# Causal attention feeding a mixture of experts: earlier closed pages, a copy moved to ScalarE, later row places, and dummy matmuls

## The chip, the cores and the metric

The kernel runs on one core of a Trainium2 chip. The metric is the device time in microseconds (us) of one execution. The engines are TensorE (PE; its weight loads are PEld), VectorE (DVE), ScalarE (ACT), GpSimd (POOL) and SyncE (SP, which here issues transfers).

## What is computed

Blockwise causal attention, whose output goes through a mixture of experts with one expert for each token:

```python
B, H, S, D = 8, 8, 576, 64
scores = q @ k.transpose(0, 1, 3, 2) / sqrt(D)
mask = pos[:, None] // 64 >= pos[None, :] // 64       # causal by blocks of 64
attn = softmax(where(mask, scores, -1e9))
x = (attn @ v).transpose(0, 2, 1, 3).reshape(B * S, H * D)   # 4608 tokens x 512
logits = x @ w_gate                                   # 8 experts
e = argmax(logits, axis=1); gate = softmax(logits)[e]
# tokens sorted by expert; for each expert: y = relu(x @ w1[e]) @ w2[e]
out = gate * y                                        # in the tokens' order
```

Inputs and output are float32.

## The kernel before

Attention works on pairs of heads: 4 pairs in a batch, 32 pairs in all, numbered p. Keys, queries and probabilities are turned on TensorE with fp16 operands. When a batch is done, its tokens are routed: VectorE chooses each token's expert (choose), TensorE ranks the tokens of each expert by matmuls with triangular ones, VectorE works out the row of each token (route), and GpSimd scatters the rows to a buffer in device memory, `xsorted`, that is divided into pages of 128 rows with one expert each. A page is closed when it is full. Afterwards 36 to 43 pages are fetched one by one, each multiplied by its expert's two matrices, and its rows are scattered to the output. The first 10 pages to be worked on (`FIRST`) are closed pages, so that they may start before the last batches have been scattered. TensorE's, ScalarE's and, in attention, GpSimd's orders are those of the program; VectorE's and SyncE's are set by a scheduler.

The turning of k (n = 1) and q (n = 0), with who copies them out of PSUM:

```python
def trans(p, n):
    ps = o_ps.tile([128, 640], F16, name=("o1", "o0")[n])
    for c in range(5):
        nc.tensor.transpose(ps[:, c * 128:c * 128 + 128], ...)      # L208
    copy = nc.scalar.copy if n else nc.vector.tensor_copy
    copy(qkT[:, n, 0:512]..., ps[:, 0:512]...)                      # L211
    copy(qkT[:, n, 512:576], ps[:, 512:576])                        # L213
```

`scores` (L231, L238) makes the scores of the next pair, and ScalarE their exponentials (L241, L233); `sums` adds the probabilities over keys on VectorE (L247, L253, L255); `attend` multiplies them by v (L272); `denominators` reads the sums on TensorE (L285) and copies the result (dl, L301); `finish` turns the pair's output (L315, L318) and divides it (L320 to L331). The PSUM pool `t_ps`, from which the tiles named tp of route, denominators and finish come, has two buffers.

```python
def route(b):
    nc.scalar.activation(ex, d, AF.Exp)
    rk_ps = psum_small()[:, 0:6 * E]
    nc.tensor.matmul(out=rk_ps..., lhsT=before16, rhs=oh...)        # L377
    ...                                                             # five more, L381
    nc.vector.reduce_sum(out=sm, in_=ex, axis=AX.X)
    nc.vector.reciprocal(x16.bitcast(F32)[:, :, 256], sm)
    nc.vector.tensor_copy(rk..., rk_ps)                             # L388
    # some 20 operations on 128x8 and 128x40 on VectorE, L392 to L429:
    # counts, pages, rows (slot), the last open pages (lastA), pages used

def scatter(b, j):                      # 128 rows of 1032 bytes
    if b == B - 2:
        nc.gpsimd.memset(spare, 0.0)
    ins = nc.gpsimd.indirect_dma_start(out=xsorted[:, :], ...)      # L442
    (early if b < B - 1 else late).append(ins.ins.name)
    ...
```

The loop over the pairs (cut), and what follows it:

```python
load(0), load(1), load_v(0), gate_weights()
for n in range(8):
    nc.tensor.matmul(out=idle[:, 0, 0:128], lhsT=ident32, rhs=ident32, ...)   # L566
cast(0); trans(0, 0); trans(0, 1); cast(1)
for t in range(4): scores(0, t)
for n in range(2): trans(1, n)
...
for p in range(PAIRS):
    load_v(p + 2); load(p + 3); cast(p + 2)
    if p == 1: route_constants()
    sums(p)
    scores(p + 1, 0); scores(p + 1, 1)
    ...                                           # scatters of the last batch
    attend(p, (0, 1), 0); attend(p, (0, 1), 1); attend(p, (2, 3, 4), 1)
    scores(p + 1, 2); scores(p + 1, 3)
    trans(p + 2, 1); trans(p + 2, 0)
    if p > HP and p % HP == 1: route(p // HP - 1)
    if p == PAIRS - 2: first_places()
    if p == PAIRS - 1: orders()                   # order1, L535
    denominators(p)
    ...                                           # scatters, load_weights
    if p: finish(p - 1)
    if p >= HP and p % HP == 0: choose(p // HP - 1)
    if p == PAIRS - 3: closed()
    if p == PAIRS - 2: free_rows()
load_weights(4 * E - 2); load_weights(4 * E - 1)  # 512 KB each, L124
for e in range(E): fill_rows(e)                   # L477
...
for T in range(5): mload(T)                       # fetch page T, L666
mtx(0)                                            # turn page 0, L676, L680
for T in range(ends[0] - 1): step(T, ends[0])

def mload(T):
    xs = xsp.tile([128, ROW], I32, name="xs")     # in the memory of the probabilities
    page = number(T, 0, ET.SP, NP - 1)            # from order1 for T < FIRST
    ins = nc.sync.dma_start(out=xs, in_=xs_pages[:, ds(page, 1), :]...)
    wait_for(ins, early if T < FIRST else early + fills + late)

def step(T, n):                                   # cut
    m1(T)                                         # first matrix, L692, relu L697
    if T == 0: finish(PAIRS - 1, yps); choose(B - 1)
    if T == 1: route(B - 1); scatters of batch 7; last_experts()
    if T == 3: last_order()
    mtx(T + 1); mth(T - 1); m2(T - 2)             # L704, L714; scale L717, scatter L718
```

Of the kernel before, what the change touches and what calls it, by code (L numbers as in the profile page):

```python
# [22 lines left out]
def kernel(  # L23
# [10 lines left out]
    nc = tc.nc  # L34
# [29 lines left out]

    FIRST = 10
# [7 lines left out]
    cnt, pages, lastA, used = (consts.tile([128, w], F32, name=n) for n, w in (  # L73
        ("cnt", E), ("pages", E), ("lastA", E), ("used", 1)))
# [14 lines left out]
    def constants():  # L89
        nc.gpsimd.memset(fill, 0)  # L90
        nc.gpsimd.iota(fill[:, 257:258], pattern=[[0, 1]], base=NO_TOKEN,
                       channel_multiplier=0)
    def route_constants():
        make_upper_triangular(nc, before16, 1.0, diag=False)
        nc.gpsimd.memset(ones16, 1.0)
        nc.gpsimd.memset(ione, 1.0)
        place_i = place.bitcast(I32)
        pref_i = pref.bitcast(I32)
        nc.gpsimd.iota(pref_i, pattern=[[0, 5], [-1, E]], base=E, channel_multiplier=0)
        nc.gpsimd.tensor_copy(pref, pref_i)  # L100
        nc.gpsimd.iota(page_i, pattern=[[0, 1]], base=0, channel_multiplier=1)
        nc.gpsimd.tensor_copy(page_f, page_i)
        nc.gpsimd.iota(place_i, pattern=[[1, NP]], base=0, channel_multiplier=0)
        nc.gpsimd.tensor_copy(place, place_i)
        nc.gpsimd.tensor_copy(page_h, page_f)
        nc.gpsimd.tensor_scalar(row_m, page_f, -128.0, None, op0=ALU.add)
        nc.gpsimd.tensor_scalar(row_n, page_f, -float(NO_TOKEN), None, op0=ALU.add)
        nc.gpsimd.memset(em_all, 0.0)
        for t in (cnt, pages, lastA, used):
            nc.gpsimd.memset(t, 0.0)  # L110
# [17 lines left out]
    with tc.tile_pool(name="ld", bufs=2) as ld, \  # L128
# [73 lines left out]
        def trans(p, n):  # L202
            if ("qkT", p) not in st:
                st["qkT", p] = c16.tile([128, 2, 576], F16, name="qkT")
            qkT = st["qkT", p]
            ps = o_ps.tile([128, 640], F16, name=("o1", "o0")[n])
            for c in range(5):
                nc.tensor.transpose(ps[:, c * 128:c * 128 + 128],  # L208
                                    h16[:, n, c].rearrange("p h d -> p (h d)"), ident16)
            copy = nc.scalar.copy if n else nc.vector.tensor_copy  # L210
            copy(qkT[:, n, 0:512].rearrange("d (p c) -> d p c", c=4),  # L211
                 ps[:, 0:512].rearrange("d (c p) -> d p c", c=4))
            copy(qkT[:, n, 512:576], ps[:, 512:576])  # L213
# [158 lines left out]
        def route(b):  # L372
            d, x16, oh = st.pop(("d", b)), st.pop(("x16", b)), ohs[b % 2]
# [6 lines left out]
            for s in range(1, 6):  # L380
# [3 lines left out]
            sm = small("sm", 5)  # L384
            nc.vector.reduce_sum(out=sm, in_=ex, axis=AX.X)
            nc.vector.reciprocal(x16.bitcast(F32)[:, :, 256], sm)
            rk = rp.tile([128, 6, E], F32, name="rk")
            nc.vector.tensor_copy(rk.rearrange("p j e -> p (j e)"), rk_ps)  # L388

            cnt2, pages2, new, inc, base, pb, tmp = (  # L390
                small(n) for n in ("cnt2", "pages2", "new", "inc", "base", "pb", "tmp"))
# [27 lines left out]
            nc.vector.tensor_copy(slot, sl)  # L419
            st["slot", b], st["x16", b] = slot, x16  # L420
# [7 lines left out]
            nc.vector.tensor_copy(cnt, cnt2)  # L428
            nc.vector.tensor_copy(pages, pages2)  # L429
# [6 lines left out]
        def scatter(b, j):  # L436

            slot, x16 = st["slot", b], st["x16", b]
            m = 128 if j < 4 else 64
            if b == B - 2:  # L440
                nc.gpsimd.memset(spare, 0.0)
            ins = nc.gpsimd.indirect_dma_start(  # L442
                out=xsorted[:, :],
                out_offset=bass.IndirectOffsetOnAxis(ap=slot[0:m, j:j + 1], axis=0),
                in_=x16[0:m, j, :], in_offset=None)
            (early if b < B - 1 else late).append(ins.ins.name)
            if b < B - 1:
                apart("rows", ins)
            else:

                wait_for(ins, fills)
                apart("end rows", ins)
                tc.add_to_no_dep_group("last rows", ins.ins)

        def free_rows():

            got, w = small("got"), small("frw")
            nc.vector.scalar_tensor_tensor(out=got, in0=pages, scalar=-128.0, in1=cnt,
# [26 lines left out]
        def closed():  # L485

            cur, hit = small("cur"), small("hit")
            opn, cl = small("opn", 1), small("cl", 1)
# [69 lines left out]
        with tc.manual_schedule(engines={ET.PE, ET.Activation, ET.Pool}):  # L558
# [5 lines left out]
            idle = s_ps.tile([128, 2, 512], F32, name="s")  # L564
            for n in range(8):
                nc.tensor.matmul(out=idle[:, 0, 0:128], lhsT=ident32, rhs=ident32, start=True,  # L566
                                 stop=True)
            cast(0)
            for n in range(2):
                trans(0, n)  # L570
            cast(1)
            for t in range(4):
                scores(0, t)
            for n in range(2):
                trans(1, n)
            load(2)
# [3 lines left out]
            for p in range(PAIRS):  # L580
# [11 lines left out]
                sums(p)  # L592
                if nxt:
                    scores(p + 1, 0)
                    scores(p + 1, 1)
                if p == PAIRS - 2:
                    scatter(B - 2, 0)
                    scatter(B - 2, 1)
                elif p == PAIRS - 1:
                    scatter(B - 2, 4)  # L600
                elif p > HP and p % HP in (2, 3):
                    scatter(p // HP - 1, 2 * (p % HP - 2))
                if p > HP + 1 and p % HP == 0:
                    scatter(p // HP - 2, 4)
# [11 lines left out]
                if p == PAIRS - 2:  # L616
                    first_places()
                if p == PAIRS - 1:
                    orders()
                denominators(p)  # L620
                if p == PAIRS - 2:
                    scatter(B - 2, 2)
                    scatter(B - 2, 3)
                elif p > HP and p % HP in (2, 3) and p < PAIRS - 2:
                    scatter(p // HP - 1, 2 * (p % HP - 2) + 1)
                if 2 < p < PAIRS - 2:
                    for n in range(((p - 3) * 30 + 26) // 27, ((p - 2) * 30 + 26) // 27):
                        load_weights(n)
                if p:
# [4 lines left out]
                if p == PAIRS - 3:  # L634
                    with tc.high_priority():
                        closed()
# [3 lines left out]
            load_weights(4 * E - 2)  # L640
            load_weights(4 * E - 1)
# [7 lines left out]
        yps.extend(t_ps.tile([128, Dm], F32, name="tp") for _ in range(2))  # L649
# [13 lines left out]
        def mload(T):  # L663
# [4 lines left out]
            if T < FIRST:  # L668
                tc.declare_no_dep(ins.ins, group="last rows", reason="pages closed before")
# [56 lines left out]
        def step(T, n):  # L726
# [5 lines left out]
            if T == 1:  # L732
                route(B - 1)
                for j in range(5):
# [33 lines left out]
        with tc.manual_schedule(engines={ET.PE, ET.Activation}):  # L768
            for T in range(5):
                mload(T)  # L770
            mtx(0)
            for T in range(ends[0] - 1):
# [35 lines left out]
```

## Time and profile before

| | before |
|---|---|
| median of 3 runs | 418.81 us (418.07 to 419.86) |
| span of the profile | 418.9 us |
| PE busy | 385.4 us (92%) |
| PEld busy | 241.8 us (58%) |
| DVE busy | 237.1 us (57%) |
| ACT busy | 212.4 us (51%) |
| POOL busy | 198.7 us (47%) |
| mean granted TensorE clock | 0.976 |

In the lines of the profile, L272 is line 272 of the kernel. A line of the timeline has the start in us, the time in us from the first to the last of the merged instructions, engine, line, operation, out<-in, how many, and in brackets how long the engine was idle before and what ended that wait. SPq is the queue of SyncE, which issues transfers. A slice of the page is a fortieth of the span; its digit is the busy share in tenths. Attention takes the span from its start to about 237 us, the experts the rest.

### The profile page before, as it was taken

What the parts mean: (1) busy time and instruction counts of PE and PEld (TensorE: products, weight loads), DVE (VectorE), ACT (ScalarE), POOL (GpSimd) and SP (SyncE); (2) the same over time, 40 slices, a digit from 0 to 9 for tenths busy, and PEclk for the clock granted to TensorE, in tenths of its full rate; (3) what the DMA queues carried; (4) which work ended last, traced back from release to release, by engine and by line L of the source; (5) the groups of instructions that cost most, each with busy time, mean ns of one, the idle gap of its engine ahead of it and who ended that gap; (6) DMA issues with size and microseconds to landing.
All of it is one profiled execution on the core that took longest, in us unless ns stands there. A gap on an engine that the chain in (4) does not pass through costs nothing.

```text
span 418.9 us, 11629 instructions
## 1 busy us (share of the span) xinstructions
PE 385.4 (92%) x4110; PEld 241.8 (58%) x4110; DVE 237.1 (57%) x767; ACT 212.4 (51%) x341; POOL 198.7 (47%) x400
## 2 busy tenths in 40 slices
PE   5999989999999899999998648999999999999993
PEld 4557656667666566576665424555555555555551
DVE  1466898897988888969889607232323232222220
ACT  4666756666667566575666002344444434343441
POOL 3565467657476676765773840612121212121212
PEclk9699999999999999999999959999999999999998
DMA  6786999989989899999894570332223222322222
GB/s 165 230 228 174 224 245 198 240 192 239 236 198 271 210 231 256 254 210 255 186 220 87 103 201 0 121 115 89 102 77 101 78 102 80 112 89 89 81 90 76
DMA packets 83067, 67.58 MB, mean 161 GB/s; under 512 B 52079, under 2 KB 75375, under 8 KB 83008
## 3 DMA queue, kind: packets, MB, share of 16 engines
q0 software_dynamic: 9824, 31.31, 32.6%
q1 hardware_dynamic: 72352, 34.89, 31.0%
q8 instruction: 37, 0.61, 0.6%
q10 hardware_dynamic: 832, 0.59, 0.5%
q14 instruction: 22, 0.18, 0.2%
HBM read 67.56 MB, written 17.23 MB: 202 GB/s over the span
## 4 chain that ended last, share of the span: by engine, by line
PE 30%; issue 28%; DVE 14%; DMA 12%; POOL 11%; ACT 2%; SPq 1%; POOLq 1%; ACTq 0%
PE o L272 14%; POOL out_dram L718 8%; PE tp L285 6%; DMA out_dram<-y,xs 4%; PE s L238 4%; DMA wall<-in_moe_w_dram 4%; PE o L208 2%; PE tp L318 2%; PE tp L315 2%; DVE acc L247 2%; DVE x L326 2%; DVE acc L253 2%; POOL xsorted L477 2%; DVE acc L255 1%; DMA qk<-in_k_dram 1%
## 5 line engine op out<-in xcount | busy, mean ns | idle before, releaser
L241 ACT ACTIVATE pt<-s 128x1024 f32<-128x1024 f32 x96 | 94.9, 1025 | 48.2 <-issue 26.9
L272 PE MATMUL o<-pt,v 128*64 128x320 f32 (+3 forms) x768 | 91.7, 389 | 0.0
L718 POOL DMA_INDIRECT out_dram<-y,xs x38 | 37.4, 983 | 111.0 <-ACT y L717 108.1
L680 DVE COPY xsT<-o 128x512 f16<-128x512 f16 x38 | 16.1, 423 | 105.9 <-PE o L676 105.8
L692 PE MATMUL s<-wall,xsT 128*128 x304 | 73.5, 386 | 2.6 <-DMA xsorted<-fill,frows 1.2
L272 PEld LDWEIGHTS o<-pt,v 128*64 128x64 f32 x768 | 50.9, 139 | 36.6 <-issue 7.3
L714 PE MATMUL tp<-wall,hT 128*128 x304 | 71.7, 379 | 0.0
L697 ACT ACTIVATE h<-s 128x1024 f16<-128x1024 f32 x38 | 38.9, 1023 | 58.5 <-PE s L692 58.5
L442 POOL DMA_INDIRECT xsorted<-x,slot x40 | 44.9, 1122 | 30.1 <-DVE em_i L504 14.1
L717 ACT ACTIVATE y<-tp,xs 128x512 f32<-128x512 f32 x38 | 26.1, 687 | 53.4 <-PE tp L714 53.4
L243 POOL MEMSET pt<- 64x128 f32 x128 | 23.8, 202 | 61.7 <-ACT pt L241 49.0
L692 PEld LDWEIGHTS <-xsT 128*128 128x128 f16 x304 | 30.1, 99 | 39.1 <-issue 2.6
L198 POOL CAST qk<-qk 128x512 f16<-128x512 f32 x62 | 44.9, 745 | 8.9 <-DMA qk<-in_q_dram 5.3
L714 PEld LDWEIGHTS <-hT 128*128 128x128 f16 x304 | 28.4, 99 | 27.1
L276 ACT COPY oT<-o 128x256 f32<-128x256 f32 x64 | 25.7, 402 | 32.6 <-PE o L272 32.6
L247 DVE TENSOR_TENSOR acc<-pt 128x896 f32<-128x896 f32 x32 | 38.2, 1195 | 2.4 <-POOL pt L243 2.4
L211 DVE COPY qkT<-o 128x512 f16<-128x512 f16 x32 | 21.9, 686 | 25.4 <-PE o L208 25.4
L238 PE MATMUL s<-qkT 64*128 64x512 f16 (+4 forms) x320 | 32.5, 298 | 2.6 <-ACT qkT L211 1.7
L285 PE MATMUL tp<-acc,picks 128*32 128x128 f32 (+1 forms) x512 | 28.3, 265 | 3.7 <-DVE acc L255 1.7
L326 DVE TENSOR_TENSOR x<-tp,rec 128x512 f16<-128x512 f32 x64 | 31.1, 485 | 0.0
L707 DVE COPY hT<-o 128x1024 f16<-128x1024 f16 x38 | 26.2, 690 | 7.3 <-PE o L704 4.8
L253 DVE TENSOR_TENSOR acc<-acc,pt 128x640 f32<-128x640 f32 x32 | 28.2, 882 | 0.0
(155 smaller groups left out, 545.8 us busy)
## 6 DMA issues: line engine op xcount, KB each, us to landing
wall<-in_moe_w_dram POOLq DMA_DIRECT2D x32, 512.0 KB, 7.4
qk<-in_q_dram SPq DMA_DIRECT2D x32, 256.0 KB, 4.5
v<-in_v_dram SPq DMA_DIRECT2D x64, 128.0 KB, 5.9
qk<-in_k_dram SPq DMA_DIRECT2D x30, 256.0 KB, 5.0
xs<-xsorted SPq DMA_DIRECT2D x43, 129.0 KB, 2.0
xsorted<-fill SPq DMA_DIRECT2D x1, 1419.0 KB
tl<-in_q_dram SPq DMA_DIRECT2D x32, 32.0 KB, 6.3
v<-in_v_dram SPq DMA_DIRECT2D x32, 32.0 KB, 5.9
```

What stands on the lines that cost most here:

```text
L198: eng.tensor_copy(h16[:, n, 0:4].rearrange("p c h d -> p h c d"), qk[:, n].rearrange("p h (c d) -> p h c d", c=4))
L238: nc.tensor.matmul(out=sp[:, h, o:o + w], lhsT=qkT[r, 1, c * 128:c * 128 + 128], rhs=qkT[r, 0, q0:q0 + w], start=True, stop=True)
L241: nc.scalar.activation(pt[:, :, t * 512:t * 512 + 512], sp, AF.Exp, scale=scale)
L247: ins = nc.vector.tensor_tensor(out=acc[:, :, 0:448], in0=pt[:, :, 128:576], in1=pt[:, :, 576:1024], op=ALU.add)
L272: nc.tensor.matmul(out=o[h * 64:h * 64 + 64, q0 - lo:hi - lo], lhsT=vt[:, c, h, :], rhs=src, start=(c == 0), stop=(c == last), skip_group_ ...
L285: nc.tensor.matmul(out=ps[32 * t:32 * t + 32, cols], lhsT=lhsT, rhs=src, start=start, stop=True, skip_group_check=True)
L326: nc.vector.tensor_tensor(out=x16[:, j:j + n, hp * 128:hp * 128 + 128].rearrange("p i (h d) -> p i h d", h=2), in0=rows.rearrange("p (i h ...
L442: ins = nc.gpsimd.indirect_dma_start(out=xsorted[:, :], out_offset=bass.IndirectOffsetOnAxis(ap=slot[0:m, j:j + 1], axis=0), in_=x16[0:m, ...
L692: nc.tensor.matmul(out=hp[:, half * 512:half * 512 + 512], lhsT=xT[:, c * 128:c * 128 + 128], rhs=weight(T, 2 * c + half), start=(c == 0), ...
L697: nc.scalar.activation(h, hp, AF.Relu)
L714: nc.tensor.matmul(out=yp, lhsT=hT[:, f * 128:f * 128 + 128], rhs=weight(T, 8 + f), start=(f == 0), stop=(f == 7))
L718: ins = nc.gpsimd.indirect_dma_start(out=out[:, :], out_offset=bass.IndirectOffsetOnAxis(ap=xs[:, 257:258], axis=0), in_=y, in_offset=None ...
```

## The change

It does five things. The first ten pages are those closed when batch 5 (of 0 to 7) has its places, not batch 6: `closed`, `first_places` and `orders` move three to four pairs forward, and batch 6's scatters are no longer waited for by the first ten fetches. ScalarE, not VectorE, copies the turned q from pair 2 on, and also the ranks. The row places become a function of their own, `places`, a pair behind the ranks, with counts and pages in two buffers in turn so that two copies fall away. A batch's five scatters go three in one pair and two in the next, where they were two, two and one; the weights are issued ahead of the attention of a pair, two in each of the last three pairs, where the last two came behind the loop. And single dummy matmuls are put between the first transposes and scores, into a tile of `t_ps`. The finish of pair 30 moves behind the turning of the first page. It is meant to take waits away where attention gives way to the experts, to take work from VectorE where it is fullest, and to keep TensorE's clock up at the start.

The diff, cut:

```diff
+    cnts, pagess = ([consts.tile([128, E], F32, name=f"{n}{i}") for i in range(2)]
+                    for n in ("cnt", "pages"))
@@ constants(), ahead of the loop; was in route_constants(), in pair 1
+        for t in (cnts[0], pagess[0], lastA, used):
+            nc.gpsimd.memset(t, 0.0)
@@ trans
-            copy = nc.scalar.copy if n else nc.vector.tensor_copy
+            copy = nc.scalar.copy if p > 1 or n else nc.vector.tensor_copy
@@ route
-            sm = small("sm", 5)
-            nc.vector.reduce_sum(out=sm, in_=ex, axis=AX.X)
-            nc.vector.reciprocal(x16.bitcast(F32)[:, :, 256], sm)
             rk = rp.tile([128, 6, E], F32, name="rk")
-            nc.vector.tensor_copy(rk.rearrange("p j e -> p (j e)"), rk_ps)
+            nc.scalar.copy(rk.rearrange("p j e -> p (j e)"), rk_ps)
+            st["rk", b] = rk, ex
+
+        def places(b):
 ... the operations on places, with sm and its reciprocal behind slot
-            nc.vector.tensor_copy(cnt, cnt2)
-            nc.vector.tensor_copy(pages, pages2)
@@ scatter
-            if b == B - 2:
+            if b < B - 1:
                 nc.gpsimd.memset(spare, 0.0)
-            (early if b < B - 1 else late).append(ins.ins.name)
+            (early if b < B - 2 else late).append(ins.ins.name)
             if b < B - 1:
                 apart("rows", ins)
+                if b == B - 2:
+                    tc.add_to_no_dep_group("last rows", ins.ins)
@@ start
-            idle = s_ps.tile([128, 2, 512], F32, name="s")
-            ... 8 dummy matmuls
+            idle = t_ps.tile([128, 512], F32, name="tp")
+            warm(8)
             cast(0)
             for n in range(2):
                 trans(0, n)
+                warm(1)
             cast(1)
             for t in range(4):
                 scores(0, t)
+                warm((0, 2, 1, 0)[t])
             for n in range(2):
                 trans(1, n)
+            warm(1)
@@ loop, after sums(p)
+                if p > HP and p % HP == 2:
+                    places(p // HP - 1)
@@ loop, after scores(p + 1, 1)
-                ... two scatters at p % HP == 2 and 3, one at 0, here and after denominators
+                if p > HP and p % HP == 3:
+                    scatter(p // HP - 1, 0)
+                    scatter(p // HP - 1, 1)
                 if p > HP + 1 and p % HP == 0:
-                    scatter(p // HP - 2, 4)
+                    scatter(p // HP - 2, 3)
+                if p > 2:
+                    first = p - 3 + max(0, p - PAIRS + 3)
+                    for n in range(first, first + 1 + (p >= PAIRS - 3)):
+                        load_weights(n)
@@ loop, around denominators(p)
-                if p == PAIRS - 2:
+                if p == PAIRS - 5:
                     first_places()
-                if p == PAIRS - 1:
+                if p == PAIRS - 4:
                     orders()
                 denominators(p)
+                if p > HP and p % HP == 3:
+                    scatter(p // HP - 1, 2)
+                if p > HP + 1 and p % HP == 0:
+                    scatter(p // HP - 2, 4)
-                if p:
+                if 0 < p < PAIRS - 1:
                     finish(p - 1)
-                if p == PAIRS - 3:
-                    with tc.high_priority():
-                        closed()
+                if p == PAIRS - 6:
+                    closed()
@@ behind the loop
-            load_weights(4 * E - 2)
-            load_weights(4 * E - 1)
+            for j in (3, 4):
+                scatter(B - 2, j)
             for e in range(E):
                 fill_rows(e)
@@ experts
             if T == 1:
                 route(B - 1)
+                places(B - 1)
@@
             mtx(0)
+            finish(PAIRS - 2)
+            yps.extend(t_ps.tile([128, Dm], F32, name="tp") for _ in range(2))
```

## The prediction

> **What bounds the kernel now.** I read the page's 40 slices first, then the busy time by stretch, then the timeline of the stretches where TensorE is not busy. The page gives TensorE 92% of the span, so only stretches in which it idles or runs at a lower granted clock, and pairs longer than its own work, can yield time.
>
> ```profile
> PE   5999989999999899999998648999999999999993
> PEclk9699999999999999999999959999999999999998
> ```
>
> There are two places with both faults: slices 1 and 2, and slices 23 to 25. By stretch (us, then busy us and count of PE, PEld, DVE, ACT, POOL, then clock, DMA share, GB/s):
>
> ```profile
> 10.00:16.80 6.80, 6.04 (x36) 3.45 (x37) 3.08 (x5) 4.20 (x8) 4.09 (x21) 0.50 0.68 175
> 238.70:242.10 3.40, 0.00 (x0) 0.00 (x0) 0.02 (x1) 0.00 (x0) 2.85 (x6) 1.00 1.06 212
> 242.10:252.30 10.20, 5.95 (x23) 3.50 (x23) 0.74 (x4) 1.02 (x1) 4.14 (x7) 0.50 0.60 180
> 98.26:104.75 6.49, 6.49 (x96) 4.51 (x94) 5.00 (x14) 4.53 (x9) 4.89 (x11) 1.00 1.06 228
> 104.75:112.07 7.32, 6.88 (x102) 4.77 (x100) 6.83 (x27) 4.63 (x10) 4.15 (x12) 1.00 1.09 233
> 112.07:119.40 7.33, 7.07 (x95) 4.63 (x93) 6.93 (x34) 4.55 (x9) 3.86 (x8) 1.00 0.91 228
> ```
>
> The reader is to see: half clock for 6.8 us at the start; 3.4 us with TensorE wholly idle between attention and experts and then 10.2 us at half clock; and three neighbouring pairs of heads, a plain one of 6.49 us, all TensorE, and two of 7.3 us in which VectorE is at 93 to 95%. The plain pair is the floor; the two long ones carry choose and route. The timeline of the change from attention to experts says why TensorE stops:
>
> ```profile
> 235.39 0.17 DVE L535 CAST order<-tp 1x20 int32<-1x20 f32 x1
> 235.50 1.18 POOL L124 DMA_DIRECT2D wall<-in_moe_w_dram  x2
> 237.28 9.22 SPq L666 DMA_DIRECT2D xs<-xsorted  x10
> 245.15 0.61 PE L676 MATMUL o<-ident,xs 128*128 128x128 f16 x4 [7.72 <-DMA xs<-xsorted]
> 246.96 3.57 PE L692 MATMUL s<-wall,xsT 128*128 x8 [1.20 <-DMA xsorted<-fill,frows]
> ```
>
> The first page is fetched only after the order of pages is known (L535) and batch 6's rows have been scattered; the fetch goes out at 237.28, behind 1 MB of weights issued at 235.5, and TensorE waits until 245.15. At the start, one more wait, and one pair's ScalarE against TensorE for later:
>
> ```profile
> 24.88 0.17 DVE L405 SCALAR_TENSOR_TENSOR room<-pages,cnt 128x8 f32<-128x8 f32 x1 [3.53 <-POOL pages L110]
> 25.84 0.41 PE L285 MATMUL tp<-acc,picks 128*32 128x128 f32 x2 [0.79 <-DVE acc L253]
> 102.61 0.27 ACT L233 ACTIVATE pf<-s 64x128 f32<-64x128 f32 x1
> 102.91 0.58 ACT L211 COPY qkT<-o 128x512 f16<-128x512 f16 x1
> 103.39 0.22 ACT L213 COPY qkT<-o 128x64 f16<-128x64 f16 x1
> 104.69 1.94 ACT L241 ACTIVATE pt<-s 128x1024 f32<-128x1024 f32 x2 [1.09 <-issue]
> 104.21 0.61 PE L238 MATMUL s<-qkT 64*128 64x512 f16 x6
> ```
>
> **What the Trainium skill says.** "TensorE: Matmul & The Clock Gate", Part 1, has the array's clock halved after an idle window of about 3.4 us and restored after a busy one, in free-running windows. The trace agrees: half clock comes in stretches of 6.8 and 10.2 us, two and three such windows. It shows more: the window of 6.6 to 10.0 us, which ended in the first half clock, had TensorE busy about 1.4 us (0.4 before 7.0, 0.61 at 7.67, 0.40 at 9.17), so some 42% was not enough. "DMA: Bandwidth & Descriptors", section "Issuing engines are not separate DMA queues", says that all transfers share the same 16 engines: the trace has the page fetches (129 KB) landing in 2.0 us at the median of the whole run, but in 6.0 us here beside the weights, with the DMA share at 1.06.
>
> **The change part by part.**
>
> *Start.* Six dummy matmuls go into the first gaps. The first eight took 3.79 us, 0.47 each, and six of 0.47 lie in gaps of 0.47, 0.68, 0.90, 0.52 and 0.68 us (TensorE's waits at 6.44, 7.67, 9.17, 10.09 and 12.19), so they displace next to nothing. The window of 6.6 to 10.0 then has 1.4 + 3 x 0.47 = 2.8 us of work, 83%, and I expect the clock to hold. At half clock the transposes of pair 1 took 1.25 us against 0.73 later, its scores 1.03 against 0.61, the attention of pair 0 4.59 against 2.81: 2.7 us. Some is lost again because the casts of pair 2 end at 16.2: its transposes can start there instead of at 18.14, so 1.9 us earlier. Then the wait on L405: the zeroing of the counters moves ahead of the other constants, and VectorE no longer stands behind it; TensorE waited 0.79 and 0.19 us, and pair 1 took 8.1 us (20.76 to 28.85) against 6.5, so about 1.4 more. Together -3.3 us.
>
> *Pairs with routing.* The copy of the turned q (0.69 + 0.17 us on VectorE) and the copy of the ranks go to ScalarE, and the some 20 small operations on row places come one pair later, behind the sums L253 and L255, on which TensorE waits. In the second long pair TensorE then no longer waits for the sums: 7.33 becomes about 6.6 (the places, some 17 operations at 0.1 us apart as in the trace, end about when the denominators do). In the first long pair VectorE's chain from the logits to the one-hot is unchanged, so the rank matmuls still wait. A new wait appears: the ranks' PSUM tile is read by ScalarE behind both copies. At 108.04 exp starts, the k copy at 109.40, q then at 110.1, the exp of d at 110.7, the ranks until 111.15; the pool gives finish's first tile the buffer of the denominators instead, which is free when dl is copied, 110.7. That is 0.45 us later than finish began (110.25), of which the old wait for dl (until 111.05) gives half back: 7.32 becomes 7.55. The two take 14.15 instead of 14.65 here. This batch is a mild one: from the sums of one batch to those of the next the chain of waits has 28.39, 27.68, 28.14, 28.49, 28.43 and 27.91 us, mean 28.2, against 27.7 for the batch I worked through, and a busier VectorE is what differs. I take 0.75 us for each of 7 batches: -5.3 us.
>
> *Plain pairs.* ScalarE gets 0.7 us more: k at 102.91, q at 103.6, its first 512 columns done at 104.17. The next scores started at 104.21. With 0.06 us from copy to matmul (12.13 to 12.19 at the start) they start at 104.23. So 0.02 us in each of some 20 pairs: +0.5 us. ScalarE's work in a pair grows from 4.53 to 5.3 of 6.5 us.
>
> *Attention to experts.* The first ten pages are now those closed after batch 5; order1 is ready three pairs before the end, and the fetches wait for batch 5's scatters and for the tiles of pair 30, whose memory they reuse, not for batch 6. So the fetch goes out about when pair 31 begins and lands while it runs, ahead of the last weights. TensorE from the last pair's attention, 232.19 in the old trace: attention 2.86, denominators 1.05, the page's transposes 0.4, finish of pair 30 1.1, a little for the page's copy: the first expert matmul 5.5 us after, instead of 14.77 (246.96). -9.3 us. The idle gap goes, so the clock should hold: from the first expert matmul to the fourth page's took 14.66 us (to 261.62). Without half clock the first costs 1.9 instead of 3.57 and the finish of pair 31 1.05 instead of 1.7, but then the rank matmuls wait about 1.5 us for VectorE; I come to 13.7. -0.9 us. The last weights, now issued one pair earlier than the end, are of the second expert matrix and needed only some 11 us later. The scatters and row fills on GpSimd (13 of 1.28 us) end about 17 us after that same point, as late as before, and batch 7's five follow to 26 us; the third page's output needs its y buffer at 27.5. It fits, with 2 us to spare or to lose on ScalarE, not on TensorE.
>
> *Bookkeeping.* The closed pages and first places move from pairs 29 to 31 into 26 to 28, where the same VectorE has them beside the places: +0.7 us.
>
> *Pages.* 38 pages at 4.17 us are not touched.
>
> Sum: -3.3 - 5.3 + 0.5 - 9.3 - 0.9 + 0.7 = -17.6, from 418.8 to 401.2; I say 401.5.
>
> **The rivals.** First, GpSimd becomes the bound of the change to experts: with five scatters and eight fills after the weights, batch 7's scatters and the outputs queue, and TensorE stands for the y buffer. For it: the chain of waits runs over L477 from 236.98 to 246.11. Against it: the buffers leave some 4 us. It would return 3 to 6 us: 405 to 407. Second, ScalarE becomes the bound of every pair: were the q copy 0.2 us later than I have it, 28 pairs would lose 5 to 6 us, the routing gain would be gone, and the time about 407. Against it: the idle 1.09 us before the next exp. Third, the start is limited by transfers (DMA share 1.02 from 16.8 to 24 us, with 1.4 MB of fill in it) and its 3.3 us come back as a wait for casts: 404. Fourth, the first page lands late all the same, beside weights and scatters: each us of wait costs one, and over 2 us of idleness would bring half clock back, so 405.
>
> **Range and chances.** The transition alone, 9 to 10 us, is over 2% (8.4 us); it rests on a wait that is plainly the last one there. Two rivals at once give 409. So 397 to 408 eight times in ten; faster by over 2% 0.93, within 2% 0.05, slower 0.02.
>
> **What would show it.** In the changed profile: no half clock at 10 us and none near 240; TensorE's wait for xs gone, and the first L703 matmul 5 to 6 us after the last pair's attention; no wait of L289 for acc, but one of the finish transposes for dl or rk in each first long pair; plain pairs of 6.5 us. Plain pairs of 6.7 or more, or TensorE waiting behind out_dram scatters, would make the prediction wrong.

## The result and the profile after

| | before | after |
|---|---|---|
| time, median (lowest to highest) | 418.93 us (418.07 to 419.86) | 407.75 us (406.33 to 409.39) |
| ratio | 1 | 0.973, 95% interval 0.969 to 0.978 |
| profiled span, mean granted clock | 418.9 us, 0.976 | 406.8 us, 0.990 |
| start of attention of pair 3 | 35.34 us | 32.56 us |
| start of attention of pair 31 | 232.19 us | 227.42 us |
| first expert matmul | 246.96 us | 235.58 us |

The kernel is 11.2 us faster; 17.4 were forecast. The page of the kernel after, its 40 slices:

```profile
PE   7899999899899899998998789999999999999992
PEclk9999999999999999999999989999999999999997
```

The two dips of before, in slices 1 to 2 and 23 to 25, are nearly gone; what is left is a shallow one in slice 23. Next the busy time by stretch of the kernel after, columns as before: the start, then the plain pair, the first and the second long pair (the same three pairs of heads, 12 to 14, that were shown of before).

```profile
10.00:16.80 6.80, 5.96 (x80) 4.32 (x81) 3.16 (x6) 5.34 (x9) 4.50 (x25) 1.00 0.65 163
94.35:100.84 6.49, 6.49 (x95) 4.54 (x94) 4.67 (x12) 5.13 (x11) 5.96 (x13) 1.00 0.97 220
100.84:108.98 8.14, 6.73 (x102) 4.78 (x100) 6.54 (x19) 5.32 (x13) 4.86 (x12) 1.00 1.08 239
108.98:115.73 6.75, 6.58 (x95) 4.51 (x93) 6.65 (x33) 5.17 (x11) 4.10 (x10) 1.00 1.02 224
```

The start holds full clock (1.00 where 0.50 stood). The plain pair is as long as ever, 6.49 us. The second long pair came down from 7.33 to 6.75, but the first went *up*, from 7.32 to 8.14, although VectorE does less in it (6.54 us busy instead of 6.83). TensorE waits more there than before. In this batch the two long pairs together got longer, from 14.65 to 14.89 us. It was a mild one before: over all seven batches the long pairs went from 105.8 to 103.7 us. TensorE's waits that matter here, over the whole run (us in total, times, longest):

```profile
PE tp L381 <- DVE oh L372: 6.7, 8, 0.9
PE tp L319 <- DVE dl L305: 3.4, 7, 0.5
PE o L687 <- DMA xs<-xsorted: 2.3, 1, 2.3
```

These are the two waits of the first long pairs, for the one-hot and for the denominators, and the wait for the first page. The timeline of the kernel after around that page:

```profile
223.60 1.07 POOL L128 DMA_DIRECT2D wall<-in_moe_w_dram  x2
225.45 4.59 SPq L677 DMA_DIRECT2D xs<-xsorted  x6
...
228.91 1.17 POOL L128 DMA_DIRECT2D wall<-in_moe_w_dram  x2
...
233.85 0.41 PE L687 MATMUL o<-ident,xs 128*128 128x128 f16 x4 [2.30 <-DMA xs<-xsorted]
235.58 3.18 PE L703 MATMUL s<-wall,xsT 128*128 x8
```

The fetch goes out 12 us earlier than before, 2 us ahead of pair 31's attention at 227.42. Yet TensorE has the page only at 233.85, some 8 us after the fetch was issued: 1 MB of weights went out 2 us ahead of it and 1 MB more 3 us behind it.

The two spans differ by 12.1 us: 2.8 at the start (35.34 - 32.56), 2.0 from pair 3 to pair 31, 6.6 from pair 31 to the first expert matmul (14.77 to 8.16), 1.2 to the fourth page's (14.66 to 13.43), less 0.5 in the pages behind.

### The profile page after: what moved, and what is told of

The parts are those of the page before. It is cut to its first block, busy times and chain, and to the rows that moved or that the text cites. A ratio compares the mean times of both kernels' runs of the same rounds, so it can differ in the third digit from the quotient of the medians.

```text
span 406.8 us, 11668 instructions
## 1 busy us (share of the span) xinstructions
PE 377.9 (93%) x4122; PEld 241.4 (59%) x4122; DVE 220.0 (54%) x683; ACT 231.2 (57%) x409; POOL 204.0 (50%) x430
## 4 chain that ended last, share of the span: by engine, by line
issue 26%; PE 25%; DMA 16%; POOL 16%; DVE 12%; ACT 2%; POOLq 1%; SPq 0%; ACTq 0%; DVEq 0%
PE o L276 9%; POOL out_dram L729 8%; PE tp L289 5%; DMA out_dram<-y,xs 4%; PE s L242 3%; DMA tl<-in_k_dram 3%; POOL xsorted L447 3%; POOL qk L202 2%; DMA qk<-in_k_dram 2%; PE o L212 2%; PE tp L319 2%; DMA xs<-xsorted 2%; POOL qk L204 2%; DMA xsorted<-x,slot 2%; PE tp L322 2%
## 5 line engine op out<-in xcount | busy, mean ns | idle before, releaser
L276 PE MATMUL o<-pt,v 128*64 128x320 f32 (+3 forms) x768 | 90.0, 383 | 0.0
L447 POOL DMA_INDIRECT xsorted<-x,slot x40 | 43.4, 1085 | 10.1 <-issue 7.4
L247 POOL MEMSET pt<- 64x128 f32 x128 | 22.8, 200 | 46.2 <-ACT pt L245 34.8
L202 POOL CAST qk<-qk 128x512 f16<-128x512 f32 x62 | 41.1, 690 | 9.5 <-DMA qk<-in_q_dram 6.8
L215 ACT COPY qkT<-o 128x512 f16<-128x512 f16 x62 | 36.9, 595 | 2.8 <-PE o L212 2.1
L251 DVE TENSOR_TENSOR acc<-pt 128x896 f32<-128x896 f32 x32 | 35.7, 1116 | 2.3 <-POOL pt L247 2.2
L305 DVE COPY dl<-tp 128x192 f32<-128x192 f32 x32 | 11.4, 355 | 47.1 <-PE tp L289 47.0
L257 DVE TENSOR_TENSOR acc<-acc,pt 128x640 f32<-128x640 f32 x32 | 35.2, 1099 | 0.1
```

Of the source, the lines that this page charges most:

```text
L202: eng.tensor_copy(h16[:, n, 0:4].rearrange("p c h d -> p h c d"), qk[:, n].rearrange("p h (c d) -> p h c d", c=4))
L215: copy(qkT[:, n, 0:512].rearrange("d (p c) -> d p c", c=4), ps[:, 0:512].rearrange("d (c p) -> d p c", c=4))
L251: ins = nc.vector.tensor_tensor(out=acc[:, :, 0:448], in0=pt[:, :, 128:576], in1=pt[:, :, 576:1024], op=ALU.add)
L257: nc.vector.tensor_tensor(out=acc[:, :, 128:448], in0=acc[:, :, 128:448], in1=pt[:, :, 1024:1344], op=ALU.add)
L276: nc.tensor.matmul(out=o[h * 64:h * 64 + 64, q0 - lo:hi - lo], lhsT=vt[:, c, h, :], rhs=src, start=(c == 0), stop=(c == last), skip_group_ ...
L447: ins = nc.gpsimd.indirect_dma_start(out=xsorted[:, :], out_offset=bass.IndirectOffsetOnAxis(ap=slot[0:m, j:j + 1], axis=0), in_=x16[0:m, ...
```

## The experiments

A pair's length is from the start of its attention to that of the next; "first" and "second" long pairs are those with p % 4 = 1 and 2, from pair 5 on. The transition is the time from the start of pair 31's attention to the first expert matmul. The runs of a set were made on one chip. The kernel before takes 419.0 us on the chip of the second set, but 428.5 and 428.2 us on those of the first and third, so ratios are always to the kernel before on the same chip, and lengths are compared within a set or between the first and third.

| run | set | median us | ratio to before, 95% interval |
|---|---|---|---|
| fifth scatter later | 1 | 421.97 | 0.984 [0.978, 0.989] |
| ranks on VectorE | 1 | 416.72 | 0.973 [0.969, 0.977] |
| weights early | 1 | 427.39 | 0.997 [0.992, 1.001] |
| no dummies | 1 | 422.33 | 0.986 [0.982, 0.989] |
| changed kernel again | 2 | 406.41 | 0.971 [0.966, 0.976] |
| fifth scatter earlier | 2 | 403.38 | 0.961 [0.956, 0.967] |
| and ranks on VectorE | 2 | 405.46 | 0.966 [0.961, 0.971] |
| and weights early | 2 | 408.06 | 0.975 [0.970, 0.981] |
| fifth scatter earlier, weights by pair 30 | 3 | 423.40 | 0.986 [0.982, 0.991] |
| q on VectorE | 3 | 418.25 | 0.978 [0.975, 0.981] |
| places at once | 3 | 423.99 | 0.990 [0.987, 0.993] |
| closed by batch 6 | 3 | 424.19 | 0.990 [0.988, 0.993] |

**Why the first long pair grew: the suspect.** In its timeline, kernel after, GpSimd's casts of the next q and k (L202) lie beside VectorE's long sum (L257):

```profile
100.25 1.32 POOL L447 DMA_INDIRECT xsorted<-x,slot  x1 [0.17 <-issue]
101.57 1.18 POOL L202 CAST qk<-qk 128x512 f16<-128x512 f32 x2
101.93 1.51 DVE L257 TENSOR_TENSOR acc<-acc,pt 128x640 f32<-128x640 f32 x1
105.70 0.18 PE L381 MATMUL tp<-oh,before 128*128 128x40 f16 x1 [0.92 <-DVE oh L372]
107.52 0.66 PE L319 MATMUL tp<-ident,oT 128*128 128x128 f32 x4 [0.49 <-DVE dl L305]
...
110.13 0.81 DVE L257 TENSOR_TENSOR acc<-acc,pt 128x640 f32<-128x640 f32 x1
```

The fifth scatter, at 100.25, now stands behind the denominators of the pair before and pushes the casts to 101.57. The sum takes 1.51 us instead of the 0.81 that it takes with no cast beside it (the last line, from the next pair), and the chain to the one-hot, which runs on VectorE behind it, ends 0.6 us later in the pair than it did before; TensorE waits 0.92 us for it (0.29 in the same pair before). The Trainium skill ("SBUF — State Buffer", section "Who interferes with whom") has it that a VectorE instruction with two inputs in SBUF contends with a GpSimd instruction that reads SBUF; the trace agrees, with 0.70 us more on 0.81.

**Fifth scatter later** (set 1).

```diff
-                if p > HP + 1 and p % HP == 0:
-                    scatter(p // HP - 2, 4)      # behind the denominators
...
+                if p > 2 * HP and p % HP == 1:
+                    scatter(p // HP - 2, 4)      # ahead of the attention
```

> The changed kernel, with a batch's fifth scatter moved one pair later, to the pair with the ranks, so that GpSimd's casts start earlier in that pair. Theory A (GpSimd's casts and VectorE's sum L257 block each other because two scatters before the casts push these into it): in the six or seven first long pairs L257 falls from 1.5 us to 0.8, the rank matmuls wait about 0.6 us less, these pairs go from 8.14 to about 7.5 us, the time falls by 2.5 to 4 us to about 404. Theory B (the pair is long because of the waits for dl and the ranks' place alone): L257 may change, the pair stays at 8.1, the time at 407.5.

First long pairs from pair 9 to 25 took 7.46 to 7.52 us, where the run without dummies, its neighbour with the routing untouched, has 8.02 to 8.15; L257 took 0.81 to 0.87 in them. But the second long pairs took 7.3 to 8.5 (6.5 to 6.8 in the neighbour, and 8.1 in pair 26), with 0.7 us and more of waiting for the denominators. So the late casts cost some 0.6 us, and this place for the scatter gives as much back a pair later: from pair 5 to 31 it takes 188.8 us, its neighbour 188.2. The two had to be parted by another place, below.

**Ranks on VectorE** (set 1).

```diff
-            nc.scalar.copy(rk.rearrange("p j e -> p (j e)"), rk_ps)
+            nc.vector.tensor_copy(rk.rearrange("p j e -> p (j e)"), rk_ps)
```

> The changed kernel, with the ranks copied by VectorE again. Theory A (the ranks' copy stands behind two q and k copies on ScalarE, so that the finish takes the other PSUM buffer and waits for dl): the wait of 0.49 us of the first finish transpose for dl goes in seven pairs, of which 0.2 us come back as the old wait for dl in the third part: the time falls by about 2 us to 405.5. Theory B (the wait is hidden behind the rank wait or VectorE): no change, 407.5.

First long pairs 7.6 to 8.0 us (pair 9 on), second 6.49, against 8.0 to 8.1 and 6.76 of its neighbour: 3.5 us less over the pairs. It looked as if the copy on ScalarE were a cost. But in pair 5, where no scatter stands in the way of the casts, it is worse, 8.27 us against 7.93. That called for the run with the scatter out of the way, below.

**Weights early** (set 1): all 32 weight transfers issued by pair 28, as in the diff of "and weights early" below.

> The changed kernel, with all weights issued by pair 28 instead of two in each of the last three pairs. Theory A (the first page lands 7.4 us after its issue because 2 MB of weights share the transfer engines with it): it lands in 2 to 3 us, TensorE's wait of 2.3 us for it goes, the clock is not halved at 235, and the time falls by 3 to 4 us to about 404. Theory B (the fetch is held by what it waits for, batch 5's scatters or the tiles of pair 30): the wait stays, 407.5.

Half an answer: TensorE does not wait for the page any more (2.3 us in the changed kernel), but it stood 9.7 us for the last pair's denominators, which VectorE had copied late (see the last section), and the transition took 18.9 us. It was run again in the second set.

**No dummies** (set 1): the six `warm(...)` calls behind the first are left out.

> The changed kernel without the six dummy matmuls between the first transposes and scores. Theory A (they hold the clock): half clock returns from 10 to 16.8 us and the time rises by 2.5 to 3 us to 410.5. Theory B (the start is bound by transfers, or the earlier zeroing of the counters brought the gain): the time stays within 1 us of 407.75.

Half clock is back at the start, in the stretch that has 1.00 with dummies:

```profile
10.00:16.80 6.80, 5.74 (x36) 3.16 (x36) 3.54 (x6) 3.83 (x7) 3.99 (x24) 0.53 0.68 180
```

Attention of pair 2 starts at 27.80, in the other three runs of the set at 25.37 to 25.97, so 1.8 to 2.4 us later; a pair later 1.7 to 2.2 of it are left. Pair 1 takes 6.49 us here too (8.09 before), so the earlier zeroing of the counters, which stays in, takes TensorE's wait out of it apart from the clock. But pair 0 takes 8.66 us (7.61 before), and of the 1.6 us only 1.05 are left where pair 2 starts (27.80 instead of 28.85).

**The changed kernel again** (set 2), unedited.

> The changed kernel once more, unedited, so that the edits beside it have a twin on the same chip. Its ratio to the kernel before was 0.973 [0.969, 0.978]. If the pairs of heads of 7.3 us where 6.5 were before, and the 8 us stall of VectorE before the last denominators, which all four experiments of the first set show, belong to the edits, this run has neither (attention of pair 5 to pair 31 in 181.9 us, first expert matmul 8.2 us after the last attention, ratio 0.973). If they belong to the chip or the run, it may have them too.

181.2 us from pair 5 to 31, transition 7.47 us, none of the odd lengths that all four edits of the first set have: those came with the chip, not with an edit. Its pair 21 is a trial made by chance:

```profile
156.38 1.79 POOL L202 CAST qk<-qk 128x512 f16<-128x512 f32 x2
156.76 0.95 DVE L257 TENSOR_TENSOR acc<-acc,pt 128x640 f32<-128x640 f32 x1
```

The second of the two casts began 0.27 us after the sum, just behind the first cast's end, where it begins 0.2 us after it, ahead of that end, in the five sister pairs behind a scatter. Now the cast waited and not the sum: L257 took 0.95 us, the two casts 1.79 instead of 1.18. This first long pair took 7.70 us, its sisters 8.13 to 8.15.

**Fifth scatter earlier** (set 2).

```diff
                 if p > HP + 1 and p % HP == 0:
                     scatter(p // HP - 2, 3)
+                    scatter(p // HP - 2, 4)
...
-                if p > HP + 1 and p % HP == 0:
-                    scatter(p // HP - 2, 4)
```

> The fifth scatter of a batch goes ahead of the attention, beside the fourth, so that GpSimd's casts for the next pairs are not pushed into the first long pair's long sum. Theory (casts against the sum): the sum L257 of the pair with the routing takes 0.81 us instead of 1.5, the wait for the one-hot falls from 0.9 to about 0.3 us, and the first long pair from 8.14 to about 7.5, 0.6 us in each of six batches: 3.6 us less than the changed kernel on the same chip, ratio to it 0.991. Rival (the chain on VectorE from the logits to the one-hot is simply as long as it was, and the copies on ScalarE set the pair): L257 shortens and the pair stays over 8 us.

The timeline of the same pair in this kernel:

```profile
100.82 1.17 POOL L202 CAST qk<-qk 128x512 f16<-128x512 f32 x2
...
101.58 1.08 DVE L257 TENSOR_TENSOR acc<-acc,pt 128x640 f32<-128x640 f32 x1
...
104.93 0.18 PE L381 MATMUL tp<-oh,before 128*128 128x40 f16 x1 [0.50 <-DVE oh L372]
...
106.75 0.66 PE L319 MATMUL tp<-ident,oT 128*128 128x128 f32 x4 [0.49 <-DVE dl L305]
```

The casts start 0.33 us after the attention instead of 0.73, only their tail meets the sum, and the wait for the one-hot falls from 0.92 to 0.50. First long pairs 8.14 to 7.73, second 6.75 to 6.49, from pair 5 to 31 177.8 us instead of 181.2: 3.3 us where the theory gave 3.6, but 2.2 of them from the first long pairs and 1.4 from the second, for which it gave nothing (the rest lost 0.2). The rival is out for this part; the wait of 0.49 for `dl`, which stays, is the part that it has right. By the medians 3.0 us are gained on the changed kernel. It is the fastest version of this study.

One relation ties these runs together. In the nine runs with the ranks and the turned q on ScalarE, on all chips, a first long pair ends 5.53 to 5.56 us after L257 does, in 62 of 63 pairs (pair 21 above has 5.65). L257 ends 1.91 us after the attention's start in pair 13 of the run with the scatter later, which takes 7.46; 2.18 and 7.72 here; 2.60 and 8.14 in the changed kernel. So what delays this sum lengthens the pair by as much. In pair 5, which no scatter precedes, the casts come earlier and meet VectorE's sum before it (L251, 1.33 us instead of 1.08): 2.39 and 7.93.

**And ranks on VectorE** (set 2): both edits.

> The same, and the copy of the ranks back on VectorE. In the first set the ranks on VectorE alone had first long pairs of 7.7 us and second ones of 6.49 where the neighbours on that chip had 8.0 and 6.76. Theory (two separate costs): they add up, first long pairs about 7.1, second 6.5, some 6 us less than the changed kernel on the same chip, ratio to it 0.985. Rival (one wait hides the other): no shorter than the better of the two alone, 3.5 us.

The second long pairs keep 6.49, the first become 8.27, and 1.8 us are lost from pair 5 to 31. The timeline says where:

```profile
105.75 0.21 DVE L389 COPY rk<-tp 128x48 f32<-128x48 f32 x1 [0.38 <-PE tp L385]
...
105.86 1.21 POOL L202 CAST qk<-qk 128x512 f16<-128x512 f32 x2
105.99 0.49 DVE L396 TENSOR_TENSOR cnt<-cnt,rk 128x8 f32<-128x8 f32 x1
...
106.52 0.58 DVE L398 TENSOR_SCALAR pages<-cnt 128x8 f32<-128x8 f32 x1
...
107.82 0.34 DVE L305 COPY dl<-tp 128x192 f32<-128x192 f32 x1
...
108.22 0.33 PE L322 MATMUL tp<-ident,oT 128*128 128x128 f32 x1 [0.88 <-DVE dl L305]
```

With the ranks ready at 105.96, the first row places (L396 and on) run on VectorE *ahead* of the copy of the denominators, and here they meet the casts: 0.49 and 0.58 us for two that take 0.17 each in the same pair of the run of the first set, where these casts begin 6.24 us after the attention's start instead of 4.89, with the places already done. TensorE waits 0.88 us for the denominators. With the ranks on ScalarE `dl` is copied ahead of the places. So the slower copy is the better one where the casts are early, as in pair 5 of the first set's run; neither theory nor rival had that.

**And weights early** (set 2): both edits and

```diff
-                if p > 2:
-                    first = p - 3 + max(0, p - PAIRS + 3)
-                    for n in range(first, first + 1 + (p >= PAIRS - 3)):
+                if 2 < p < PAIRS - 3:
+                    for n in range((p - 3) * 32 // 26, (p - 2) * 32 // 26):
                         load_weights(n)
```

> The same, and the last eight weight transfers spread over the pairs before, all issued by pair 28. Theory (the first page lands late because it shares the transfer engines with the last 2 MB of weights): from the last attention to the first expert matmul 5.5 to 6 us instead of 8.2, half clock gone there, 3 us less than without it. Rival (the first page waits for the scatters and for its own descriptors): nothing gained there. Second rival (the weights then crowd the loads of heads, whose casts come late): pairs of 6.49 become 6.8 and more, and 2 to 4 us are lost.

Theory and second rival both hold. Stretches from the last attention to the first expert matmul, and on to the fourth page's, of this kernel:

```profile
230.49:235.81 5.32, 5.26 (x76) 3.86 (x76) 3.78 (x11) 0.80 (x2) 4.65 (x7) 1.00 0.73 195
235.81:247.86 12.05, 10.03 (x75) 6.02 (x73) 9.72 (x53) 3.19 (x4) 9.97 (x19) 1.00 0.30 93
```

5.32 us with TensorE busy 5.26 of them, and a share of the transfer engines of 0.73. The changed kernel on the same chip has

```profile
226.02:233.49 7.47, 5.34 (x77) 3.87 (x77) 3.80 (x11) 0.80 (x2) 6.33 (x13) 1.00 1.05 242
233.49:245.53 12.04, 10.01 (x75) 6.02 (x73) 9.58 (x52) 3.28 (x5) 7.78 (x15) 1.00 0.69 176
```

with a share of 1.05: TensorE does the same 5.3 us of work and waits for the rest, which is the page. But the weights, crowded into the pairs, make TensorE wait for casts of late loads; its waits over the run:

```profile
PE o L212 <- POOL qk L202: 6.4, 8, 2.7
```

From pair 5 to 31 it is 5.6 us slower than the run without this edit, about what the transition and the full clock behind it give back (9.07 to 5.32, and 14.10 to 12.05 from the first expert matmul to the fourth page's); by the medians 2.6 us are lost.

**Fifth scatter earlier, weights by pair 30** (set 3): four weight transfers in pair 29, two in pair 30, none in pair 31.

> The fifth scatter beside the fourth, and the last six weight transfers where no loads of heads are left to crowd: four in pair 29, two in pair 30, none in pair 31. Theory (the first page shares the transfer engines with the last weights; the pairs suffer only where weights meet loads of heads): from the last attention to the first expert matmul 5.4 to 6 us as with all weights early, pairs as with the fifth scatter earlier (177.8 us from pair 5 to 31), so 2 to 3 us less than that one's 403.4: about 401, ratio to the kernel before 0.955. Rival (the last loads of v and casts are still crowded): pairs 29 and 30 over 8 and 6.5 us, nothing gained.

Partly shown, and the total left open; the ratio leaves out one of the six times, 428.9 us, in which the granted clock was lower than in the others. The page was in time: TensorE waited 0.46 us for it (2.0 in the changed kernel of set 2), and for casts 1.2 us in the whole run. Pairs 29 and 30 took 7.79 and 5.95 us, so its rival is out. But then, as in the first set, the last denominators came late, and the transition took 10.36 us:

```profile
238.56 0.41 PE L686 MATMUL o<-ident,xs 128*128 128x128 f16 x4 [0.46 <-DMA xs<-xsorted]
242.99 0.36 DVE L305 COPY dl<-tp 128x192 f32<-128x192 f32 x1 [6.30 <-remote]
243.41 0.33 PE L322 MATMUL tp<-ident,oT 128*128 128x128 f32 x1 [3.39 <-issue]
```

What this version takes on a chip like that of the second set was not measured.

**q on VectorE** (set 3).

```diff
-            copy = nc.scalar.copy if p > 1 or n else nc.vector.tensor_copy
+            copy = nc.scalar.copy if n else nc.vector.tensor_copy
```

> The changed kernel with the copy of the turned q back on VectorE. Theory (VectorE bounds the pairs with routing, its 0.86 us a pair are what the change saves): first long pairs from 8.14 to 8.5 or more, second from 6.75 to about 7.2, plain ones 6.49; 4 to 7 us more than the changed kernel, ratio to the kernel before 0.984 to 0.99. Rival (ScalarE is as tight as VectorE now): it gives back in the first long pair, where the copies of k, q, exp and ranks stand in a row before finish, what it takes in the second; within 1 us of the changed kernel.

**Places at once** (set 3): `places(p // HP - 1)` right behind `route(p // HP - 1)`.

> The changed kernel with the row places computed right behind the ranks again, not a pair later. Theory (the places beside the sums lengthen the second long pair): second long pairs from 6.75 back to 7.2 or more, some 3 us more in all, ratio to the kernel before about 0.98. Rival (the scheduler orders VectorE by need, so the place in the program changes little): within 1 us of the changed kernel.

The two long pairs of the third batch by stretch. With q on VectorE:

```profile
103.00:110.58 7.58, 6.78 (x101) 4.76 (x99) 6.95 (x24) 4.76 (x11) 4.27 (x10) 1.00 1.05 223
110.58:117.89 7.31, 6.58 (x95) 4.51 (x93) 7.28 (x36) 4.56 (x9) 4.10 (x11) 1.00 0.94 205
```

With the pages closed by batch 6, whose routing is that of the changed kernel:

```profile
103.22:111.37 8.15, 6.73 (x102) 4.78 (x100) 6.55 (x19) 5.33 (x13) 5.01 (x12) 1.00 1.03 212
111.37:118.13 6.76, 6.59 (x96) 4.51 (x94) 6.66 (x33) 5.17 (x11) 4.10 (x10) 1.00 1.03 229
```

With the places at once:

```profile
111.19:118.53 7.34, 7.08 (x95) 4.64 (x93) 6.93 (x35) 5.16 (x11) 3.70 (x10) 1.00 1.00 221
```

The q copy on ScalarE takes 0.55 us off the second long pair, in which VectorE would be busy without a gap (7.28 of 7.31 us), and puts 0.57 on the first. Of that 0.13 is the casts (L257 ends 2.48 us after the attention's start with q on VectorE, 2.61 with it on ScalarE); the other 0.44 lie behind the sum, where exp, both copies and the ranks stand in a row on ScalarE: the pair ends 5.10 us after L257 and not 5.54. So the theory of q on VectorE is out and its rival holds: by the pairs' lengths that part of the change is worth about 0.1 us a batch as it stands. The medians can't say it: the set has no run of the changed kernel itself, and VectorE's late copies (last section) fall ahead of the first expert matmul in its other runs and behind it in this one (transition 6.17 us). With the scatter earlier, q on VectorE was not run. The places a pair later are what shortens the second long pair: 7.34 to 6.76, 0.58 us per batch, with the first little changed (8.02, where L257 ends at 2.49, and 8.15, where it ends at 2.61).

**Closed by batch 6** (set 3): the first ten pages are those closed after batch 6, and their order is made in pair 31.

> The changed kernel with its first ten pages closed by batch 6 again, all else kept. Theory (the earlier choice of pages is what starts the experts sooner): the first page's fetch goes out only when the order is known and batch 6's rows are scattered, from the last attention to the first expert matmul 13 to 15 us instead of 7.5 to 8.2, and half clock for about 10 us behind it; 6 to 8 us more than the changed kernel, ratio to the kernel before about 0.988. Rival (the page is late because of weights and scatters whatever pages are chosen): 9 to 10 us, 2 us more.

The timeline of this kernel, when the order is known and when the page is there:

```profile
237.20 0.17 DVE L542 CAST order<-tp 1x20 int32<-1x20 f32 x1 [0.25 <-PE tp L540]
...
248.66 0.61 PE L684 MATMUL o<-ident,xs 128*128 128x128 f16 x4 [10.46 <-DMA xs<-xsorted]
```

The transition takes 18.49 us where the run with the places at once, on the same chip, has 13.58. TensorE waits 10.46 us for the page, 2.07 in that run, which stands 3.9 us more for the late denominators; here these come while the page is still awaited. So the 4.9 us between the two runs understate it; the wait for the page is 8.4 us longer. The theory holds in kind, and the rival, 2 us, is out. It is no return to the kernel before, though: batch 6's last two scatters stay behind the loop, the last goes out at 238.29 and the fetch at 246.98, where the kernel before had 234.02 and 237.28.

## Why the prediction was right or wrong

The direction, the place of the gain and the range were right; the sum was 5.5 us too large by the spans (17.6 against 12.1). By its own steps:

- *Start, -3.3.* Right: attention of pair 2 starts 3.41 us earlier. The dummies are worth about 2 of it: from 6.6 to 10.0 us TensorE is busy 2.64 us (78%; 2.8 were forecast), 1.30 without them, and half clock follows only there. The zeroing gave about 1, where 1.4 were forecast. 0.63 us went again in pair 2, which waits for transfers and casts: a small part of the third rival.
- *Plain pairs, +0.5.* Not needed: they are still 6.49 us. The second rival (ScalarE bounds every pair) did not come.
- *Routing pairs, -5.3, with +0.7 for bookkeeping.* The term that was most wrong in kind. The second long pair went as forecast (6.75, forecast 6.6), and by both of its causes: with the places or the q copy put back it takes 7.34 or 7.31 us. The new wait in the first was forecast and came (0.49 us for `dl`, forecast 0.45). But the step "VectorE's chain from the logits to the one-hot is unchanged" failed: its head, the sum L257, took 1.51 instead of 0.88 us beside casts that the moved fifth scatter had made late. 7.55 plus that 0.6 is the measured 8.14. Moving the scatter gave 0.4 of it back. The bookkeeping is as forecast: pair 26, which has it, takes 7.49 us where the second long pairs ahead of it take 6.75. Pairs 3 to 31 in all gained 2.0 us where these terms made 4.1.
- *Attention to experts, -9.3.* Right in kind, too large by 2.7: 8.16 us instead of 5.5. The fetch went out when the prediction said, 2 us ahead of pair 31's attention, but did not land "ahead of the last weights": it shared the transfer engines with 2 MB of them, and TensorE waited 2.30 us. The working even had 6.0 us for a fetch in this stretch before (on record for the one of 242.3, beside row fills more than weights; the first took 7.9, from 237.28 to 245.15), and did not apply it. That was the fourth rival. With no weights left at that point the transition took 5.32 us, so the 5.5 was the right sum of TensorE's work; the step that failed is the landing.
- *Half clock there, -0.9.* Measured -1.2. One window of half clock remained in this profile and none in the second run of the same kernel (13.43 and 12.04 us for the same stretch), with 2.3 and 2.0 us of idleness ahead of it.
- *GpSimd, the first rival.* Its last row fills wait 2.15 us for weights to land and batch 7's scatters follow at 248.59, but TensorE never waited for them.

## What to carry to other kernels

When an instruction is moved on an engine that looks half idle, look at what stands *behind* it in that engine's queue: a scatter that was put off made casts late, and the casts slowed a sum on another engine at the head of the chain that TensorE waits for. A fetch that is issued early enough is not yet there early enough: what was issued ahead of it and just behind it on the shared transfer engines sets when it lands, and taking those out of the way is only a gain where nothing else needs the time they move to. A faster copy can hurt when it lets less urgent work go ahead of urgent work.

## What the runs showed of the hardware that was not expected

- Two casts on GpSimd beside a two-input sum on VectorE cost some 0.7 us between them, and less than 0.1 us in the second cast's start decided which side paid: L257 took 1.51 us instead of 0.81 with the two casts at 1.18, or 0.95 with the casts at 1.79. The section named above has it that issue order decides who blocks. The trace agrees that one side waits while the other runs, but by the recorded starts the sum was ahead of the second cast both times; what differed is whether that cast had begun before the first one ended.
- The same program took 2.2 to 2.3% more on two of the chips (the kernel before 428.5 and 428.2 us instead of 419.0). In most runs there, a pair in four (p % 4 = 3) took 0.6 to 1.4 us more than 6.49, mostly with a pause inside the denominators (L289) for which the records name no releaser, and VectorE copied the last denominators 5 us and more after TensorE had made them. In the run without dummies TensorE's last denominators end at 239.65 us, and:

```profile
247.02 0.36 DVE L305 COPY dl<-tp 128x192 f32<-128x192 f32 x1 [8.38 <-remote]
247.43 0.48 PE L322 MATMUL tp<-ident,oT 128*128 128x128 f32 x1 [3.80 <-issue]
```

  The records hold transfers of instructions of 16 KB 1.6 to 4.0 us ahead of the pauses in the pairs of this run, but the runs on the other chip have such transfers without a pause. The cause stays open, and with it the time of the last version above.
